# A rebuilt prologue, and kernel sums issued one chunk behind their phase factors, in an S4 convolution with a gated FFN and its backward pass

## The chip, the core and the metric

The kernel runs on one core of one Trainium2 chip. The core has five engines with a queue each: TensorE (PE, with its weight loads shown as PEld), VectorE (DVE), ScalarE (ACT), GpSimd (POOL) and SyncE (SP). DMAs are issued from the queues of SP, ACT and POOL and share 16 DMA engines. The metric is the device time of one execution in microseconds, as the median of several runs.

## What is computed

The reference computes a block and all of its gradients. With x of 2048 rows (time) by 576 channels:

```
xn = layernorm(x)
s  = S4(xn)                 # a long convolution per channel
g  = silu(FFN(xn))          # silu(xn w1) * (xn w3), times w2, 4608 hidden
y  = x + s * g
```

The convolution's kernel is generated per channel d from 128 complex modes n:

```
P[d,n,l] = exp(dt[d] * A[d,n] * l)          # A = A_re + i A_im, l = 0..2047
K[d,l]   = Re sum_n C[d,n] P[d,n,l] dt[d] B[d,n]
```

The outputs are y and the gradients with respect to x, A, B, C, log_dt, Dskip, w1, w3 and w2 (13 arrays).

## The kernel before, in words

Each queue runs its instructions in order. A planner puts them in that order when the program is built: each instruction has a due time (set by `self.at`, which counts for all that follows it, and by program order within it), and the planner places, on a clock of its own estimates, the earliest due instruction that is ready by those estimates. So instructions of different phases interleave, and the order is fixed before the chip runs. Buffers come from pools on a stack. A pool that is opened after another was closed takes over its bytes or its PSUM banks, and its first writer waits for the last reader of the tile that was there.

**Prologue** (no `self.at`, so it is due before all else). It consists of:

- `setup_consts`: identities, constant columns, index row.
- `phase2_params`: loads dt, Dskip and the six matrices A, B, C (576 x 128 each, on 128 partitions x 5 chunks x 128). It computes rho = dt A_re, thp = dt A_im / 2 pi, and W = C B dt (Wr, Wi: ten DVE operations of 128 x 640, two of them sums). W is transposed by PE (L248) and copied by ACT (L251) to `WrT` and `nWiT`. `split_rates` cuts thr, th64 (phase rates modulo one, for steps of 1 and 64) and rho into three bf16 pieces each (L304, L307), and writes them to DRAM as `PCS_dram` with 54 DMAs, alternating between SP and ACT (L81, called from L311).
- `build_selectors`: SEL and SELR, the right-hand sides that turn rates into phases (48 of 128 rows for SELR's use), from integer ramps of POOL (L333 to L337).
- `phase1_layernorm`: 16 tiles of 128 rows are loaded by SP (L135), statistics, root and normalisation on DVE and ACT, 80 transposes on PE (L156) and ten copies out (L159 ACT, L161 DVE) to `xnT`.
- `build_dft_mats`: the 512-point DFT tables dC, dSf, dSi, by DVE and three ACT activations (L539 to L541).
- `ssm_early`: loads the rho pieces as `lhs_r` (L400). For each of 36 chunks of 16 channels, three matmuls on 48 rows of 512 columns (L408) give the exponents, one ACT exponential of 1536 columns (L410) gives the decay factors, and one DMA writes them to `E_dram` (L411). Then, for 32 groups, eight matmuls of 288 columns (L419) give the spectra of xn; DVE copies them out (L423), through a single PSUM buffer, and eight DMAs write `UH_dram` (L425).

**Kernel generation** (`ssm_kernel`, 36 chunks, 8 due-time units apart). Per chunk: phase pieces `lhs_t` (L448, every sixth chunk) and E are loaded; PE makes phases (L466), DVE masks them into `m_k` (L467), ACT makes sine and cosine (`trig`, L316 to L320), DVE multiplies by E to `q_k` and `p_k` (L473, L475), POOL rearranges p into `pz_k` (L482), DVE negates a part (L483) and multiplies by W to `t_k` and `v_k` (L490 to L494). Then 64 small matmuls (L499) sum q times v over the modes into `kps`, and ACT copies that into `KT` (L502). **The FFN** (`ffn_hidden`, from L686) is due beside it: 144 steps of ten matmuls of 512 columns (L719 to L721) with copies on ACT and DVE. The convolution (`ssm_conv`) follows the last chunk; then come the FFN's output, the backward pass and the gradients, which the change leaves alone.

Of the kernel before, what the change touches and what calls it, by code (L numbers as in the profile page):

```python
# [60 lines left out]
class K:  # L61
# [24 lines left out]
    def setup_consts(self):  # L86
# [15 lines left out]
        self.zero_col = const.tile([P, 1], FP32, name="zero_col")  # L102
        nc.vector.memset(self.zero_col[:], 0.0)
# [4 lines left out]
        self.pmod64 = const.tile([P, 1], FP32, name="pmod64")  # L108
        nc.vector.tensor_scalar(out=self.pmod64[:], in0=self.pcol[:], scalar1=64.0, scalar2=-64.0,
                                op0=ALU.is_ge, op1=ALU.mult)  # L110
        nc.vector.tensor_tensor(out=self.pmod64[:], in0=self.pmod64[:], in1=self.pcol[:], op=ALU.add)
# [7 lines left out]
    def phase1_layernorm(self, xp):  # L119
        nc, cfg = self.nc, self.cfg  # L120
        L, D, LT, DT = cfg.L, cfg.D, cfg.LT, cfg.DT
        self.xn_bf = self.persist.tile([P, LT, D], BF16, name="xn_bf")
        self.rstd = self.persist.tile([P, LT], FP32, name="rstd")
        self.xnT = xp.tile([P, DT, L], BF16, name="xnT")
        xf = self.aps["A_u"].flatten_outer_dims()
        half = D // 2
        nfull = D // P
        rem = D - nfull * P
        with self.tc.tile_pool(name="ln_sb", bufs=1) as sb, self.tc.tile_pool(name="ln_small", bufs=4) as small, \
                self.tc.tile_pool(name="ln_ps", bufs=2, space=bass.MemoryType.PSUM) as ps:  # L130
            xs = []
            mv = sb.tile([P, LT, 2], FP32, name="mv")
            for i in range(LT):
                xt = sb.tile([P, D], BF16, name=f"xt{i}")
                nc.sync.dma_start(out=xt[:], in_=xf[i * P:(i + 1) * P, :])  # L135
                xs.append(xt)
                stats = small.tile([P, 2, 6], FP32, name="stats")
                nc.vector.bn_stats(stats[:, 0, :], xt[:, 0:half])
                nc.vector.bn_stats(stats[:, 1, :], xt[:, half:D])
                nc.vector.bn_aggr(mv[:, i, :], stats[:])  # L140
            sd = sb.tile([P, LT], FP32, name="sd")
            nc.scalar.activation(out=sd[:], in_=mv[:, :, 1], func=ACT.Sqrt, bias=self.eps_col[:], scale=1.0)
            nc.vector.reciprocal(out=self.rstd[:], in_=sd[:])
            negmr = sb.tile([P, LT], FP32, name="negmr")
            nc.vector.scalar_tensor_tensor(out=negmr[:], in0=mv[:, :, 0], scalar=-1.0, in1=self.rstd[:], op0=ALU.mult,
                                           op1=ALU.mult)
            for i in range(LT):
                nc.vector.tensor_scalar(out=self.xn_bf[:, i, :], in0=xs[i][:], scalar1=self.rstd[:, i:i + 1],
                                        scalar2=negmr[:, i:i + 1], op0=ALU.mult, op1=ALU.add)
            TB = 8  # L150
            for tb in range(0, LT, TB):
                tsl = slice(tb * P, (tb + TB) * P)
                for c, (do, dsz) in enumerate(cfg.dch):
                    pt = ps.tile([P, TB * P], BF16, name="ln_pt")
                    for j in range(TB):
                        nc.tensor.transpose(pt[:dsz, j * P:(j + 1) * P], self.xn_bf[:, tb + j, do:do + dsz],  # L156
                                            self.ident_bf[:])
                    if c % 2 == 0:
                        nc.scalar.copy(out=self.xnT[:dsz, c, tsl], in_=pt[:dsz, :])  # L159
                    else:  # L160
                        nc.vector.tensor_copy(out=self.xnT[:dsz, c, tsl], in_=pt[:dsz, :])  # L161
                nc.sync.dma_start(out=self.xnT[rem:P, nfull, tsl], in_=self.xnT[0:rem, nfull, tsl])
# [48 lines left out]
    def phase2_params(self):  # L211
        nc, cfg = self.nc, self.cfg
        D, DT, N = cfg.D, cfg.DT, cfg.N
        aps = self.aps
        self.parp_ctx = ExitStack()
        self.parp = self.parp_ctx.enter_context(self.tc.tile_pool(name="parp", bufs=1))
        pp = self.parp
        with self.tc.tile_pool(name="par_tmp", bufs=1) as tmp, \
                self.tc.tile_pool(name="par_ps", bufs=2, space=bass.MemoryType.PSUM) as ps:
# [3 lines left out]
            self.dskip_col = self.load_dvec(pp, aps["A_Dskip"], "dskip", fill=0.0)  # L223
            self.load_rates(tmp)
            dt_b = self.dt_col[:, :, None].to_broadcast([P, DT, N])
            self.rho = tmp.tile([P, DT, N], FP32, name="rho")
            nc.vector.tensor_tensor(out=self.rho[:], in0=self.A_re[:], in1=dt_b, op=ALU.mult)
            self.thp = tmp.tile([P, DT, N], FP32, name="thp")
            nc.vector.scalar_tensor_tensor(out=self.thp[:], in0=self.A_im[:], scalar=1.0 / (2 * PI), in1=dt_b,
                                           op0=ALU.mult, op1=ALU.mult)  # L230
            self.Wr = tmp.tile([P, DT, N], FP32, name="Wr")
            self.Wi = tmp.tile([P, DT, N], FP32, name="Wi")
            t1 = tmp.tile([P, DT, N], FP32, name="t1")
            t2 = tmp.tile([P, DT, N], FP32, name="t2")
            nc.vector.tensor_tensor(out=t1[:], in0=self.C_re[:], in1=self.B_re[:], op=ALU.mult)
            nc.vector.tensor_tensor(out=t2[:], in0=self.C_im[:], in1=self.B_im[:], op=ALU.mult)
            nc.vector.tensor_tensor(out=self.Wr[:], in0=t1[:], in1=t2[:], op=ALU.subtract)
            nc.vector.tensor_tensor(out=self.Wr[:], in0=self.Wr[:], in1=dt_b, op=ALU.mult)
            nc.vector.tensor_tensor(out=t1[:], in0=self.C_re[:], in1=self.B_im[:], op=ALU.mult)
            nc.vector.tensor_tensor(out=t2[:], in0=self.C_im[:], in1=self.B_re[:], op=ALU.mult)  # L240
            nc.vector.tensor_tensor(out=self.Wi[:], in0=t1[:], in1=t2[:], op=ALU.add)
            nc.vector.tensor_tensor(out=self.Wi[:], in0=self.Wi[:], in1=dt_b, op=ALU.mult)
            self.WrT = pp.tile([P, D], BF16, name="WrT")
            self.nWiT = pp.tile([P, D], BF16, name="nWiT")
            for src, dst, sc in ((self.Wr, self.WrT, 1.0), (self.Wi, self.nWiT, -1.0)):
                for c, (do, dsz) in enumerate(cfg.dch):
                    pt = ps.tile([P, P], FP32, name="pt")
# [5 lines left out]
            self.split_rates(tmp)  # L253
            self.dskip_diag = pp.tile([P, DT, P], BF16, name="dskip_diag")
            for c in range(DT):
                nc.vector.tensor_scalar(out=self.dskip_diag[:, c, :], in0=self.ident_bf[:],
                                        scalar1=self.dskip_col[:, c:c + 1], scalar2=None, op0=ALU.mult)
        self.Wr = None
        self.Wi = None
# [28 lines left out]
    def split_rates(self, tmp):  # L288
        nc, cfg = self.nc, self.cfg
        D, DT, N = cfg.D, cfg.DT, cfg.N  # L290
        self.PCS_dram = self.dram.tile([3, 3, D, N], BF16, name="PCS_dram")
        t = tmp.tile([P, DT, N], FP32, name="sr_t")
        thr = tmp.tile([P, DT, N], FP32, name="thr")
        nc.vector.tensor_scalar(out=t[:], in0=self.thp[:], scalar1=MAGIC, scalar2=-MAGIC, op0=ALU.add, op1=ALU.add)
        nc.vector.tensor_tensor(out=thr[:], in0=self.thp[:], in1=t[:], op=ALU.subtract)
        th64 = tmp.tile([P, DT, N], FP32, name="th64")
        nc.vector.tensor_scalar(out=t[:], in0=thr[:], scalar1=64.0, scalar2=MAGIC, op0=ALU.mult, op1=ALU.add)
        nc.vector.tensor_scalar(out=t[:], in0=t[:], scalar1=-MAGIC, scalar2=None, op0=ALU.add)
        nc.vector.scalar_tensor_tensor(out=th64[:], in0=thr[:], scalar=64.0, in1=t[:], op0=ALU.mult, op1=ALU.subtract)
        for q, src in enumerate((thr, th64, self.rho)):  # L300
            pc = tmp.tile([P, 3, DT, N], BF16, name=f"pc{q}")
            r = src
# [1042 lines left out]
```

## Time and profile before

| what | value |
|---|---|
| median of 3 runs | 2397.93 us (2394.15 to 2408.3) |
| the profiled execution | 2408.83 us, its span 2407.0 us |
| busy share of the span | PE 83%, DVE 63%, ACT 38%, POOL 18% |
| mean granted clock of PE | 0.895 |

The profile is of one execution. The span runs from its first to its last instruction; the profiled execution is 1.8 us longer than its span. Shares of busy time are means over stages with different limits. PEld overlaps PE. The granted clock is that of TensorE as a share of full speed. In a row of grouped instructions the figures behind the count are the total busy time and the mean of one in ns, then the idle time of the engine just before them with what ended it. Lines such as L408 are lines of the kernel before.

### The profile page before, as it was taken

What the parts mean: (1) busy time and instruction counts of PE and PEld (TensorE: products, weight loads), DVE (VectorE), ACT (ScalarE), POOL (GpSimd) and SP (SyncE); (2) the same over time, 40 slices, a digit from 0 to 9 for tenths busy, and PEclk for the clock granted to TensorE, in tenths of its full rate; (3) what the DMA queues carried; (4) which work ended last, traced back from release to release, by engine and by line L of the source; (5) the groups of instructions that cost most, each with busy time, mean ns of one, the idle gap of its engine ahead of it and who ended that gap; (6) DMA issues with size and microseconds to landing.
All of it is one profiled execution on the core that took longest, in us unless ns stands there. A gap on an engine that the chain in (4) does not pass through costs nothing.

```text
span 2407.0 us, 42210 instructions
## 1 busy us (share of the span) xinstructions
PE 2008.8 (83%) x16735; PEld 1340.2 (56%) x16790; DVE 1505.0 (63%) x2860; ACT 902.7 (38%) x1461; POOL 426.5 (18%) x691
## 2 busy tenths in 40 slices
PE   0698888788999499789888857989899996799968
PEld 0323333333455277567767745766666675577746
DVE  6414777767788345479969674866655772276751
ACT  0355777667655211254454422333344330000000
POOL 1001444444311211111111111111111111000000
PEclk9656888888899799899999977999999998899989
DMA  3145667566755888755556478667556656999884
GB/s 81 46 192 201 242 230 251 200 226 213 243 193 179 195 219 193 183 145 155 145 148 186 125 123 203 159 176 171 154 163 156 165 140 150 224 193 184 151 115 96
DMA packets 615894, 416.10 MB, mean 173 GB/s; under 512 B 420176, under 2 KB 559568, under 8 KB 610576
## 3 DMA queue, kind: packets, MB, share of 16 engines
q1 hardware_dynamic: 477728, 235.69, 40.7%
q0 software_dynamic: 29520, 109.15, 14.4%
q10 hardware_dynamic: 108448, 68.57, 10.4%
q8 instruction: 131, 2.15, 0.4%
q14 instruction: 67, 0.55, 0.1%
HBM read 130.65 MB, written 190.37 MB: 133 GB/s over the span
## 4 chain that ended last, share of the span: by engine, by line
PE 29%; DVE 13%; issue 12%; DMA 10%; SPq 4%; ACT 4%; POOL 2%; ACTq 1%; POOLq 0%; DVEq 0%
PE px L1214 10%; SPq L1091 4%; PE ph L1133 4%; PE et_ps L578 2%; DMA out_dram<-gw 2%; PE pgw L1170 2%; PE et_ps L940 2%; DMA w2T<-w2r 2%; PE et_ps L560 2%; PE pgw L1159 2%; PE pg L719 1%; PE pu L719 1%; DVE cm_t L602 1%; DVE gg_n L1119 1%; DMA gK<-gK_dram 1%
## 5 line engine op out<-in xcount | busy, mean ns | idle before, releaser
L947 DVE TENSOR_TENSOR pr_q<-et_ps,pz 128x512 f32<-128x512 f32 x288 | 186.0, 680 | 186.0 <-PE et_ps L940 185.9
L1170 PEld LDWEIGHTS <-xn_bf 128*128 128x128 bf16 x2304 | 233.4, 102 | 80.4 <-issue 43.8
L1214 PE MATMUL px<-wTB_w,ggc 128*128 128x288 bf16 x1152 | 243.1, 292 | 33.7 <-DVE gx L1217 11.0
L1214 PE MATMUL px<-wTB_w,guc 128*128 128x288 bf16 x1152 | 242.6, 291 | 23.2 <-DMA guc<-GU_dram 12.1
L719 PEld LDWEIGHTS <-xnT 128*128 128x128 bf16 x1152 | 109.7, 104 | 201.1 <-issue 113.0
L719 PE MATMUL pg<-wmB_w,xnT 128*128 128x512 bf16 x539 | 169.1, 422 | 22.0 <-ACT g_t L727 12.3
L950 DVE TENSOR_REDUCE S_all<-pr_q 128x8 f32<-128x512 f32 x288 | 184.7, 676 | 0.3
L1133 PE MATMUL ph<-w2T,goT 128*128 128x256 bf16 x1152 | 174.5, 284 | 7.2 <-DMA w2T<-w2r 6.7
L1170 PE MATMUL pgw<-gg_n,xn_bf 128*128 128x256 bf16 x1152 | 143.6, 287 | 32.9 <-ACT gw L1173 32.8
L719 PE MATMUL pu<-wmB_w,xnT 128*128 128x512 bf16 x559 | 167.5, 408 | 1.7 <-issue 0.6
L1159 PE MATMUL pgw<-go_o,h_n 128*128 128x288 bf16 x1152 | 165.7, 301 | 1.8 <-ACT gw L1163 1.8
L774 PE MATMUL po<-w2g,hc 128*128 128x288 bf16 x1152 | 146.4, 289 | 20.1 <-DMA w2g<-in_B_w_dram 20.1
L1133 PEld LDWEIGHTS <-goT 128*128 128x128 bf16 x1152 | 99.5, 100 | 96.3 <-issue 62.3
L1214 PEld LDWEIGHTS <-ggc 128*128 128x128 bf16 x1152 | 113.2, 100 | 68.9 <-issue 26.4
L1136 ACT CAST gh<-ph 128x512 bf16<-128x512 f32 x144 | 79.7, 591 | 182.1 <-DMA GU_dram<-gu_n 63.0
L1214 PEld LDWEIGHTS <-guc 128*128 128x128 bf16 x1152 | 114.4, 99 | 56.2 <-DMA guc<-GU_dram 13.5
L1170 PE MATMUL pgw<-gu_n,xn_bf 128*128 128x256 bf16 x1152 | 141.3, 281 | 3.9 <-ACT gw L1163 3.9
L1173 ACT CAST gw<-pgw 128x256 bf16<-128x256 f32 x144 | 51.2, 380 | 248.4 <-DMA out_dram<-gw 104.0
L774 PEld LDWEIGHTS <-hc 128*128 128x128 bf16 x1152 | 112.3, 99 | 50.6 <-issue 20.9
L1159 PEld LDWEIGHTS <-h_n 128*128 128x128 bf16 x1152 | 115.2, 103 | 40.7 <-issue 5.0
L733 POOL DMA_DIRECT2D G_dram<-g_t x72 | 52.5, 728 | 465.7 <-ACT g_t L727 226.5
L1231 ACT ACTIVATE t<-gx 128x576 f32<-128x576 f32 x16 | 10.9, 684 | 324.7 <-DVE gx L1217 299.5
(309 smaller groups left out, 3982.1 us busy)
## 6 DMA issues: line engine op xcount, KB each, us to landing
Q_dram<-q_k SPq DMA_DIRECT2D x36, 512.0 KB, 3.3
G_dram<-g_t POOLq DMA_DIRECT2D x72, 256.0 KB, 3.5
H_dram<-h_t SPq DMA_DIRECT2D x72, 256.0 KB, 3.4
U_dram<-u_t POOLq DMA_DIRECT2D x72, 256.0 KB, 4.0
gg_n<-G_dram POOLq DMA_DIRECT2D x18, 1024.0 KB, 5.4
h_n<-U_dram POOLq DMA_DIRECT2D x18, 1024.0 KB, 6.6
GU_dram<-gu_n ACTq DMA_DIRECT2D x144, 128.0 KB, 3.1
GG_dram<-gg_n ACTq DMA_DIRECT2D x144, 128.0 KB, 4.4
```

Of the source, the lines that this page charges most:

```text
L719: nc.tensor.matmul(pt[:], lhsT=xnT[:, c, ts], rhs=wm[w][:, c, :], start=(c == 0), stop=False)
L733: nc.gpsimd.dma_start(out=dst[fb * ng:(fb + 1) * ng, :, i0:i0 + NT, :].rearrange("g p t f -> p g (t f)"), in_=src[:].rearrange("p g t f -> ...
L774: nc.tensor.matmul(po_[:, pi_, 0:pw], lhsT=hc[:, fi, :], rhs=w2[fi][:, po:po + pw], start=(fi == 0), stop=(fi == FT - 1))
L947: nc.vector.tensor_tensor(out=pr[:], in0=T[h][:].rearrange("p r d k a -> p (r d) k a"), in1=pz[:, dg, h, s:s + 2].rearrange("p r d a -> p ...
L950: nc.vector.tensor_reduce(out=S_all[:, 2 * s:2 * s + 2, d0:d0 + 4].rearrange("p k d -> p d k"), in_=pr[:].rearrange("p (r d) k a -> p d k ...
L1091: self.nc.sync.dma_start_transpose(out=dst, in_=src)
L1133: nc.tensor.matmul(ph[j][:, k, :].rearrange("p (a f) -> p a f", f=P), lhsT=lw, rhs=rh, start=(n == 0), stop=(n == nfull))
L1136: nc.scalar.copy(out=gh[:, j], in_=ph[j][:])
L1159: nc.tensor.matmul(pgw[pi_][:, 0:pw], lhsT=hn[:, tt, fl * P:(fl + 1) * P], rhs=go_o[:, tt, po:po + pw], start=(tt == 0), stop=(tt == LT - 1))
L1170: nc.tensor.matmul(pw_[:, 0:FG], lhsT=self.xn_bf[:, tt, c * P:(c + 1) * P], rhs=nat[:, tt, :], start=(tt == 0), stop=(tt == LT - 1))
L1173: nc.scalar.copy(out=gw[:], in_=pw_[:, 0:FG])
L1214: nc.tensor.matmul(px[pi_][:, 0:pw], lhsT=act[:, fi, :], rhs=wT[part][ai][:, f, po:po + pw], start=(fi == 0 and ai == 0), stop=(fi == FT - ...
```

## The change

The prologue becomes one function, `prologue`. All of its SBUF pools are open at once, so nothing in it reuses another's bytes; two PSUM pools, for the transposes of W and of the LayerNorm, are closed before the pool of the exponentials is opened.

- Order in the program: loads of dt, the matrices and Dskip; selectors; rho and its split; the 16 input loads; the load of `LR_`; LayerNorm; DFT tables; W; exponentials; spectra; then thp, thr, th64 and their splits; dskip_diag.
- Each of the three splits writes its pieces with 6 DMAs for 18 before.
- Wr, Wi, SEL and dskip_diag move from DVE to POOL.
- The exponentials use all 128 rows, the rows from 48 on of `LR_` being set to zero by POOL. They are done in 54 activations of 1024 columns for 36 of 1536, and written with 18 DMAs for 36.
- The spectra have two PSUM buffers for one.
- In kernel generation the sum of a chunk is issued in the program behind the next chunk's instructions, and q and v get three buffers in place of two.

```diff
+            logdt = self.load_dvec(tmp, aps["A_log_dt"], "logdt", fill=0.0)
+            self.load_rates(tmp)
+            dskip_col = self.load_dvec(tmp, aps["A_Dskip"], "dskip", fill=0.0)
+            SELR = self.build_selectors(st, selp)
+            LR_ = lp.tile([P, D // 16, N], BF16, name="lhs_r")
+            nc.gpsimd.memset(LR_[:], 0.0)
...
+            mul(nc.vector, rho, self.A_re, dt_b)
+            self.split3(tmp, rho, 2)
+            self.ln_load(lsb)
+            for k in range(3):
+                nc.sync.dma_start(out=LR_[k * 16:(k + 1) * 16], in_=self.PCS_dram[2, k].rearrange("(k p) n -> p k n", p=16))
+            self.phase1_layernorm(lsb, small, lps)
+            self.build_dft_mats(matp, dg)
...
+            pl = nc.gpsimd
+            for (W, xr, xi, op) in ((Wr, self.B_re, self.B_im, ALU.subtract), (Wi, self.B_im, self.B_re, ALU.add)):
+                mul(pl, W, self.C_re, xr[:])
+                mul(pl, t1, self.C_im, xi[:])
+                pl.tensor_tensor(out=W[:], in0=W[:], in1=t1[:], op=op)
+                mul(pl, W, W, dt_b)
...
+            early.close()
+            eps = late.enter_context(pool(name="ex_ps", bufs=2, space=PS))
+            self.early_exps(SELR, LR_, ep, eps)
+            self.early_spectra(up, ups)
...
+            self.split3(tmp, thr, 0)
+            self.split3(tmp, th64, 1)
...
+        for (c, p0, n, h, d1) in self.dsplit():
+            self.dma(self.PCS_dram[q].rearrange("k (d h) n -> h d k n", h=2)[h, d1:d1 + n], pc[p0:p0 + n, :, c, :])
...
+        for c2 in range(0, NCH, 2):
+            E = ep.tile([P, 2, TW], BF16, name="E_k")
+            Ef = E[:].rearrange("p c t -> p (c t)")
+            for o in range(0, 2 * TW, 1024):
+                pe = ps.tile([P, 1024], FP32, name="e_ps")
+                for k in range(2):
+                    ch, o1 = divmod(o + 512 * k, TW)
+                    nc.tensor.matmul(pe[:, 512 * k:512 * k + 512], lhsT=LR_[:, c2 + ch, :], rhs=SELR[:, o1:o1 + 512],
+                                     start=True, stop=True)
+                nc.scalar.activation(out=Ef[:, o:o + 1024], in_=pe[:], func=ACT.Exp)
+            nc.sync.dma_start(out=self.E_dram[c2:c2 + 2].rearrange("c p t -> p c t"), in_=E[:])
...
-                self.kgen_chunk(ch, E, LT_[:, ch % GE, :], self.SEL, mp, sb, sb, ps, ps1)
...
+                qv = self.kgen_chunk(ch, E, LT_[:, ch % GE, :], self.SEL, mp, sb, qvp, ps)
+                if ch > 0:
+                    self.kgen_sum(ch - 1, prev, ps1)
+                prev = qv
+            self.at(T0 + TK * NCH)
+            self.kgen_sum(NCH - 1, prev, ps1)
```

More of the change, by code (lines that the diff above doesn't have):

```diff
@@ L128, in phase1_layernorm @@
         rem = D - nfull * P
[L129 to L162, printed above, removed]
@@ new lines, in phase1_layernorm @@
+        xs = self.xs
+        mv = sb.tile([P, LT, 2], FP32, name="mv")
+        for i in range(LT):
+            stats = small.tile([P, 2, 6], FP32, name="stats")
+            nc.vector.bn_stats(stats[:, 0, :], xs[i][:, 0:half])
+            nc.vector.bn_stats(stats[:, 1, :], xs[i][:, half:D])
+            nc.vector.bn_aggr(mv[:, i, :], stats[:])
+        sd = sb.tile([P, LT], FP32, name="sd")
+        nc.scalar.activation(out=sd[:], in_=mv[:, :, 1], func=ACT.Sqrt, bias=self.eps_col[:], scale=1.0)
@@ new lines, in phase1_layernorm @@
+        TB = 8
+        for tb in range(0, LT, TB):
+            tsl = slice(tb * P, (tb + TB) * P)
+            for c, (do, dsz) in enumerate(cfg.dch):
+                pt = ps.tile([P, TB * P], BF16, name="ln_pt")
+                for j in range(TB):
+                    nc.tensor.transpose(pt[:dsz, j * P:(j + 1) * P], self.xn_bf[:, tb + j, do:do + dsz],
+                                        self.ident_bf[:])
+                if c % 2 == 0:
+                    nc.scalar.copy(out=self.xnT[:dsz, c, tsl], in_=pt[:dsz, :])
+                else:
+                    nc.vector.tensor_copy(out=self.xnT[:dsz, c, tsl], in_=pt[:dsz, :])
+            nc.sync.dma_start(out=self.xnT[rem:P, nfull, tsl], in_=self.xnT[0:rem, nfull, tsl])
@@ L236, in phase2_params @@
[L236 to L241, printed above, removed]
@@ L364, in ssm_forward @@
+        for (sl, rr) in ((slice(0, QW), rq), (slice(QW, QW + PW), rp)):
+            nc.gpsimd.tensor_scalar(out=self.SEL[:, sl], in0=val[:, sl], scalar1=rr[:, 0:1], scalar2=rc[:, 0:1],
+                                    op0=ALU.mult, op1=ALU.add)
+        return SELR
     def ssm_forward(self, T0, TK, TC):
@@ L412, in ssm_early @@
+        if True:
             for h in range(2):
```

252 lines of the change are left out of this document (118 added, 134 removed).

## The prediction

> **What bounds the kernel now.** I read the busy time by stretch first, because the edits touch only two stages and a share of the whole span says nothing about them.
>
> ```profile
> core 0: us, PE busy (x) PEld busy (x) DVE busy (x) ACT busy (x) POOL busy (x), PEclk, DMA share, GB/s
> 0.00:86.00 86.00, 13.30 (x90) 8.56 (x90) 57.38 (x162) 18.84 (x26) 6.55 (x18) 0.95 0.25 60
> 86.00:111.60 25.60, 18.62 (x72) 10.15 (x72) 6.06 (x8) 0.14 (x1) 0.00 (x0) 0.50 0.29 57
> 111.60:204.00 92.40, 90.76 (x261) 27.37 (x261) 15.15 (x20) 53.48 (x38) 0.00 (x0) 0.50 0.46 181
> 204.00:216.00 12.00, 8.46 (x33) 4.52 (x32) 3.03 (x5) 1.21 (x1) 0.00 (x0) 0.50 0.49 169
> 225.00:620.00 395.00, 324.49 (x3194) 140.70 (x3227) 290.57 (x509) 285.09 (x374) 173.35 (x236) 0.87 0.65 223
> 634.00:820.00 186.00, 170.38 (x1128) 93.01 (x1144) 145.99 (x179) 95.53 (x208) 35.91 (x51) 0.97 0.66 192
> ```
>
> Each row is one stretch; after the five engines come the granted clock, the DMA share and GB/s. The prologue lasts to 216. Its first 86 us have no full engine: a chain. From 111.6 to 204 PE is busy throughout at clock 0.50, so PE sets the pace there. In 225:620 (kernel generation beside the FFN) no engine is full: PE 82%, DVE 74%, ACT 72%; the stage is made of waits. 634:820 is PE at 92% and is not touched.
>
> The timelines (start, length, instruction, wait) show how the prologue chain hangs together.
>
> ```profile
> 5.86 0.53 SPq L81 DMA_DIRECT2D C_im_bf<-in_A_C_im_dram  x1
> 17.75 14.79 SPq L81 DMA_DIRECT2D PCS_dram<-pc  x27
> 32.65 4.38 SPq L448 DMA_DIRECT2D lhs_t<-PCS_dram  x9
> 44.78 7.61 SPq L135 DMA_DIRECT2D xt<-in_A_u_dram  x16
> 47.06 0.46 DVE L138 BATCH_NORM_STATS2 stats<-xt 128x6 f32<-128x288 bf16 x1 [2.42 <-DMA xt<-in_A_u_dram]
> 75.50 1.01 ACT L159 COPY xnT<-ln_pt 64x1024 bf16<-64x1024 bf16 x1 [0.69 <-PE ln_pt L156]
> 84.14 2.00 ACT L541 ACTIVATE dC<-dft_q,halfpi_col 128x2048 bf16<-128x2048 f32 x1
> 86.21 1.39 SPq L400 DMA_DIRECT2D lhs_r<-PCS_dram x3
> 121.28 1.46 PE L408 MATMUL e_ps<-SELR,lhs_r 48*128 48x512 bf16 x3
> 122.67 1.14 PE L419 MATMUL u_ps<-xn_bf,dC 128*128 128x288 bf16 x4
> 123.61 0.45 PE L419 MATMUL u_ps<-xn_bf,dSf 128*128 128x288 bf16 x1
> 216.23 0.63 PE L719 MATMUL pg<-wmB_w,xnT 128*128 128x512 bf16 x1
> ```
>
> SP writes the split rates (27 DMAs, as many on ACT's queue), loads lhs_t, and only then, at 44.78, the input; LayerNorm runs 47.1 to 76.5; the DFT tables end at 86.1; the rates for the exponentials load at 86.2, when the tables' pool is free; the FFN starts at 216.2.
>
> **Part 1, start and LayerNorm.** In the new order the input DMAs depend on nothing and stand behind the parameter loads alone, which leave SP at 6.4; so the first statistics run near 9. The LayerNorm chain itself took 76.5 - 47.1 = 29.4. In front of it DVE now has the selectors and one split instead of three.
>
> ```profile
> L354 DVE SCALAR_TENSOR_TENSOR val<-dl,pm,val 128x1536 f32<-128x1536 f32 x1 | 1.8, 1818 | 0.0
> L335 DVE CAST dl<-ii 128x1536 f32<-128x1536 int32 x1 | 1.0, 961 | 1.0 <-POOL ii L334 1.0
> L227 DVE TENSOR_TENSOR rho<-A_re_bf,dt_col 128x640 f32<-128x640 bf16 x1 | 0.8, 817 | 0.0
> L304 DVE CAST pc<-rho 128x640 bf16<-128x640 f32 x1 | 0.5, 484 | 0.0
> L482 POOL COPY pz_k<-p_k 128x256 bf16<-128x256 bf16 x138 | 104.0, 796 | 27.3 <-issue 23.8 <-DVE p_k L475 3.3
> L445 POOL MEMSET lhs_t<- 128x768 bf16 x2 | 1.4, 736 | 0.0
> ```
>
> Groups by line: busy time, mean of one, idle before. Selectors: two casts 1.9, val 1.8, SELR and the column-sized ones some 2 at these rates: 6. Rate: rho and two subtractions at 0.82, three casts at 0.48: 4. So LayerNorm ends at 9 + 29.4 + 10 = **48**; at 38 if these 10 fit its gaps.
> The exponentials cannot start earlier than that: their two PSUM buffers take four of eight banks, the spectra's two take the other four, and the four are those of the LayerNorm transposes and W's, whose pools close first. "Overlap" here is the rate path, the loads and the tables, not the exponentials.
> The eight Wr/Wi products leave DVE (8 x 0.82 = 6.5) for POOL, where no row shows a two-input operation. Bounds: DVE's 0.82 each below; above, 640 columns at the copy's rate. The copy takes 796 ns for 256 strided columns, so 2.0 each and 16 in all. I take 16, since that row is POOL's own. With POOL's iotas, SEL's two products and the new LR_ memset (4608 columns; the 768-column one takes 0.74, so 4.4) they end at about 30, and the ten W transposes behind them fit before 48. If that cover fails, 8 us.
>
> ```profile
> L490 DVE TENSOR_TENSOR t_k<-p_k,WrT x36: 677/951/3045, 229.7 to 625.5; 128x1024 bf16<-128x1024 bf16 x36
> ```
>
> This DVE product takes 677 ns at best and 3045 at worst (minimum, median, maximum); POOL's copies run beside it. So W on POOL can stretch DVE's LayerNorm by up to POOL's 16: LayerNorm end 64, the upper bound. The Trainium skill, "SBUF — State Buffer", Who interferes with whom, says that DVE and GpSimd share one port pair under an exclusive lock, and the later one blocks fully. The spread in the row agrees; its time is rival 3.
>
> **Part 2, exponentials and spectra.**
>
> ```profile
> L410 ACT ACTIVATE E_k<-e_ps 128x1536 bf16<-128x1536 f32 x36 | 52.1, 1451 | 37.3 <-PE e_ps L408 37.3
> L159 ACT COPY xnT<-ln_pt 128x1024 bf16<-128x1024 bf16 x4 | 4.0, 1012 | 5.6 <-PE ln_pt L156 5.6
> L410 ACT ACT_TABLE_LOAD x1 | 1.3, 1283 | 27.1 <-PE e_ps L408 27.1
> L423 DVE CAST u_e<-u_ps 128x576 bf16<-128x576 f32 x32 | 24.2, 758 | 107.6 <-PE u_ps L419 107.6
> 840.24 12.54 PE L774 MATMUL po<-w2g,hc 128*128 128x288 bf16 x82 [18.88 <-DMA w2g<-in_B_w_dram]
> 853.95 8.86 PE L774 MATMUL po<-w2g,hc 128*128 128x288 bf16 x71 [1.17 <-DMA w2g<-in_B_w_dram]
> 268.23 1.04 PE L719 MATMUL pg<-wmB_w,xnT 128*128 128x512 bf16 x4
> 269.11 1.03 PE L719 MATMUL pu<-wmB_w,xnT 128*128 128x512 bf16 x4
> 840.00:844.00 4.00, 3.76 (x16) 2.34 (x17) 0.61 (x3) 0.00 (x0) 0.75 (x1) 0.50 1.05 362
> 844.00:848.00 4.00, 4.00 (x31) 2.88 (x29) 0.30 (x2) 0.00 (x0) 0.00 (x0) 0.92 1.04 358
> ```
>
> ACT: 54 exponentials of 1024 columns at 1.01 (the PSUM copy of that size) = 54.6; the tables' three activations about 5.8 (2.00 is dC); two table loads 2.6; six split DMAs on its queue (14.79 / 27 = 0.55 each) 3.3: **66**.
> PE at clock 0.50: from 121.28 to 122.67 three exponential matmuls, 0.46 each, and (123.61 - 122.67) / 4 = 0.235 for each of the spectra's 256: 108 x 0.46 + 256 x 0.235 = 110. At clock 1.0: 0.22 (268.23 to 269.11, four) and 8.86 / 71 = 0.125: 24 + 32 = 56.
> DMA: 0.46 x 92.4 + 0.49 x 12 = 48 us of all engines; 18 are left under ACT's 66 for the remaining split writes. DVE: 24 for the spectra and about 10 for the other two splits.
> So ACT sets the end **if the clock rises**: 48 + 66 = 114, and 4 for in-order losses: the FFN starts at 118, a gain of **98**. Does it rise? In 111.6:204 it stayed at 0.50 with PE 98% busy, but 1.39 of every 1.39 + 8 x 0.235 = 3.3 us were matmuls on 48 rows. L774, all 128 rows, went from 0.50 to 1.00 within 8 us of dense work. The change feeds all 128 rows (48 real, the rest zeros) and double-buffers the spectra's PSUM, which removes the gaps of 86:111.6. I count rows, not values, and take 1.0.
> The Trainium skill, "TensorE: Matmul & The Clock Gate", Part 1, says that about 3.4 us of sustained matmuls lift the clock, and makes no condition of how many rows they use. The 92 us at 0.50 do not agree with it; if rows indeed don't matter, what held the clock there may hold it again, and that is rival 1.
> On PE the spectra stand behind the first exponentials, and on ACT the split DMAs wait for DVE's casts with exponentials behind them; both are prices of lateness, within the 4. SP now carries 18 double-size E writes for 36, same bytes; the FFN weights wait there for the parameters' pool, whose last readers (the theta splits) are hidden by DVE's idle time in the exponentials.
> The removed constants (under 0.5 us) and dskip_diag's move to POOL (1.2 on DVE) have cover on both sides: nothing.
>
> **Part 3, sums one chunk later.**
>
> ```profile
> PE kps L499 <- DVE v_k L493: 54.7, 25, 3.9
> DVE pz_k L483 <- POOL pz_k L482: 43.1, 28, 2.3
> DVE m_k L467 <- PE et_ps L466: 25.0, 15, 3.4
> DVE q_k L473 <- ACT C_k L320: 19.1, 14, 2.4
> ```
>
> Waits in 225:620: total, times, longest. PE stands 54.7 us for the v of the same chunk; FFN matmuls and the next phase factors queue behind, and DVE then waits 25.0 for them. With sums of the previous chunk the first wait goes. DVE's waits on POOL and ACT stay, 62.2. Bounds: nothing gained (the planner still puts a sum where its v becomes ready), up to 65: all of PE's idle, 70.5, less a little. I take half of the PE wait, 27, near DVE's 25.0. q and v get a third buffer, so no new wait on them.
>
> **Sum.** The profiled run took 2408.83 (span 2407.0 and 1.8 around it): 2408.8 - 98 - 27 = 2284. It lies 10.9 above the median 2397.93; on the median's scale **2273**.
>
> **Rivals.**
> 1. The clock stays at 0.50: PE's 110 set the end, 48 + 112 = 160, gain 56: 2398 - 56 - 27 = 2315. For it: 92 busy us at 0.50. Against: L774. 0.16.
> 2. Sums are issued as early as before; no gain there: 2300. For it: the wait shows that PE's order already differs from DVE's pace. 0.15.
> 3. POOL's W products block DVE: LayerNorm ends at 64, not 48, so 2289. For it: the 3045 ns; against: DVE's statistics wait for their input at first anyway (2.42). 0.08.
> 4. It doesn't do what it says: FFN and generation are gated by a late pool, as lhs_r was by the tables. If the theta splits (10 on DVE, DMAs, weight load) run after the spectra, about 20 late: 2293; the worst of it eats the gain. 0.10.
> 5. Slower: the clock in the generation stage. Its PE work is 324.49 x 0.87 = 282 at full clock. Above 395 + 98 = 493 the gain is gone, so from a mean clock under 282 / 493 = 0.57. At 0.50: 564, so 2398 - 98 + 169 = 2469. For it: the narrow sums leave the array nearly empty, and dips to 0.50 exist; against: the idle that precedes them shrinks. 0.05.
>
> **How the numbers follow.** Forecast 0.46. Low: LayerNorm at 38 and the full 65: 2398 - 108 - 65 = 2225. High: half clock and no gain of sums, 2342, rounded to 2345; only rival 5 and the tails lie outside. A change under 0.5% (12 us) can't be told from none. Slower 0.05 (rival 5), within 0.5% 0.02 (the worst of rival 4), faster 0.93.
>
> **What would show it.** First xt load near 7, LayerNorm's last copy near 48; exponentials packed at 1.0 us each on ACT; clock 1.0 within 10 us of the spectra's start; first pg matmul near 118; the wait of PE kps on v_k below 20 and the stage some 27 shorter. Wrong if the clock stays low, if W or a split gates the first exponential, or if another DVE wait takes up the sums' place.

## The result, and the profile after

The changed kernel is faster, by about what was forecast:

| | before | after |
|---|---|---|
| median of four runs, us | 2398.92 (2394.15 to 2408.3) | 2290.56 (2281.82 to 2296.16) |
| ratio | 1 | 0.954, 95% interval 0.9496 to 0.9585 |
| span of the profiled run, us | 2407.0 | 2292.4 |
| mean granted clock in it | 0.895 | 0.922 |

The busy time by stretch comes first again, now with the bounds at which the stages of the changed kernel begin and end.

```profile
core 0: us, PE busy (x) PEld busy (x) DVE busy (x) ACT busy (x) POOL busy (x), PEclk, DMA share, GB/s
0.00:58.00 58.00, 14.58 (x90) 9.42 (x91) 45.28 (x130) 15.28 (x25) 26.33 (x32) 0.99 0.35 74
65.50:119.00 53.50, 53.44 (x320) 32.17 (x321) 19.68 (x26) 50.49 (x55) 0.94 (x2) 0.95 0.83 312
119.00:144.00 25.00, 17.56 (x80) 8.34 (x79) 7.40 (x11) 5.08 (x9) 2.15 (x3) 0.80 0.77 241
157.00:539.00 382.00, 330.00 (x3332) 143.63 (x3332) 290.03 (x508) 278.95 (x370) 184.07 (x237) 0.86 0.69 235
```

The exponentials and spectra, 92.4 us at clock 0.50 before, now take 53.5 at 0.95, with PE full and ACT at 94%. A new stretch of 25 us stands behind them, PE at 70%. The last row is the generation stage from its first sum to its last: PE 86% and clock 0.86, against 82% and 0.87 before.

The timelines of ACT, PE and DVE of the changed kernel give the landmarks (start, length, instruction, wait in front).

```profile
36.34 0.24 ACT L258 ACTIVATE nWiT<-pt 128x64 bf16<-128x64 f32 x1 [0.46 <-PE pt L255]
36.60 1.28 ACT L136 ACT_TABLE_LOAD   x1
55.24 1.91 ACT L557 ACTIVATE dSf<-dft_fr 128x2048 bf16<-128x2048 f32 x1
57.06 0.99 ACT L153 COPY xnT<-ln_pt 64x1024 bf16<-64x1024 bf16 x1
70.83 11.11 ACT L408 ACTIVATE E_k<-e_ps 128x1024 bf16<-128x1024 f32 x12 [2.07 <-PE e_ps L406]
118.11 1.07 ACT L408 ACTIVATE E_k<-e_ps 128x1024 bf16<-128x1024 f32 x1
124.40 1.42 DVE L429 CAST u_e<-u_ps 128x576 bf16<-128x576 f32 x2 [3.64 <-DMA UH_dram<-u_e]
128.98 1.67 PE L737 MATMUL pg<-wmB_w,xnT 128*128 128x512 bf16 x7
134.72 0.37 PE L738 MATMUL pg<-wtail,xnT 64*128 64x512 bf16 x1 [1.97 <-DMA wtail<-in_B_w_dram]
142.11 0.86 PE L478 MATMUL et_ps<-SEL,lhs_t 128*128 128x512 bf16 x3
```

LayerNorm's last copy ends at 58.05 (76.5 before), the exponentials are packed (12 in 11.11 us, 0.93 each) and end at 119.2, the FFN starts at 128.98 (216.2), 87 us earlier. The first phase factors come at 142.1 (215.9), only 74 earlier: behind the first FFN matmuls stand the last spectra's writes, the FFN's weights and the loads of the rates, at 0.77 of the DMA engines. From the first phase factors to the last sum it is then 396 us instead of 417, 21 less, so that the FFN's last matmul comes 96 us earlier (725.7 against 821.4). The two spans differ by 114.6 us, so 19 lie behind the FFN, where the change edits nothing. One wait of ACT there is 14.1 us shorter:

```profile
ACT gh L1136 <- DMA GU_dram<-gu_n: 37.4, 1, 37.4
```

```profile
ACT gh L1154 <- DMA GU_dram<-gu_n: 23.3, 1, 23.3
```

The first row is before, the second after (waits of the stretch; total, times, longest). These 19 us are not shown to come from the change. From the FFN's last matmul to the end of the span the traces of all eleven kernels here take 1562 to 1586 us; 1586 is the kernel before, 1567 the changed one, and one kernel with the changed prologue (both edits undone, below) takes 1584 although its longest wait there is 23.0 us.

The wait that the delayed sums should have removed is still there (waits from the first sum to the last):

```profile
PE kps L517 <- DVE v_k L505: 51.6, 23, 3.7
DVE pz_k L495 <- POOL pz_k L494: 42.7, 33, 1.7
```

It was 57.3 us before, from its own first sum to its last (54.7 in the stretch of the prediction), and is 51.6 now, and yet the stage is 21 us shorter. So two questions go to the chip: what did the delayed sums bring, and why did the clock rise in the prologue?

### The profile page after: what moved, and what is told of

Read it like the earlier page. It is cut to its first block, busy times and chain, and to the rows that moved or that the text cites. A ratio compares the mean times of both kernels' runs of the same rounds, so it can differ in the third digit from the quotient of the medians.

```text
span 2292.4 us, 42164 instructions
## 1 busy us (share of the span) xinstructions
PE 1956.9 (85%) x16790; PEld 1333.6 (58%) x16790; DVE 1498.9 (65%) x2842; ACT 900.5 (39%) x1480; POOL 459.5 (20%) x707
## 4 chain that ended last, share of the span: by engine, by line
PE 31%; DVE 16%; issue 11%; DMA 9%; SPq 4%; ACT 4%; POOL 2%; ACTq 1%; POOLq 0%; DVEq 0%
PE px L1232 10%; PE ph L1151 4%; SPq L1109 4%; PE pgw L1188 3%; PE et_ps L958 3%; PE et_ps L596 2%; PE pgw L1177 2%; DMA w2T<-w2r 2%; DVE cm_t L620 2%; DMA out_dram<-gw 2%; PE et_ps L578 2%; PE pg L737 1%; PE pu L737 1%; DVE gg_n L1137 1%; DVE pr_q L965 1%
## 5 line engine op out<-in xcount | busy, mean ns | idle before, releaser
L737 PE MATMUL pg<-wmB_w,xnT 128*128 128x512 bf16 x576 | 176.0, 425 | 12.0 <-ACT g_t L745 10.7
L737 PE MATMUL pu<-wmB_w,xnT 128*128 128x512 bf16 x576 | 172.1, 412 | 3.7 <-ACT u_t L746 3.7
L1188 PE MATMUL pgw<-gg_n,xn_bf 128*128 128x256 bf16 x1152 | 136.4, 278 | 30.2 <-ACT gw L1191 30.2
L1188 PE MATMUL pgw<-gu_n,xn_bf 128*128 128x256 bf16 x1152 | 142.1, 282 | 4.0 <-ACT gw L1181 3.9
L958 PE MATMUL et_ps<-gK,qT 64*128 64x64 bf16 x1152 | 124.6, 289 | 8.6 <-DVE pr_q L965 7.1
```

The lines of the kernel that those rows point to most:

```text
L737: nc.tensor.matmul(pt[:], lhsT=xnT[:, c, ts], rhs=wm[w][:, c, :], start=(c == 0), stop=False)
L958: nc.tensor.matmul(T[h][:, 1 - k, dd].rearrange("p k (f t) -> p k f t", f=2), lhsT=qT[hs, k, d8, :], rhs=gK[hs, :, :, :, cc * 8 + d8].rear ...
L1188: nc.tensor.matmul(pw_[:, 0:FG], lhsT=self.xn_bf[:, tt, c * P:(c + 1) * P], rhs=nat[:, tt, :], start=(tt == 0), stop=(tt == LT - 1))
```

## Experiments

Ratios are against the kernel before in the same session; 0.001 of it is 2.4 us. The changed kernel's own is 0.954.

**The sums, undone alone.** Everything of the change stays, but each sum is issued within its chunk.

```diff
-                if ch > 0:
-                    self.kgen_sum(ch - 1, prev, ps1)
-                prev = qv
-            self.at(T0 + TK * NCH)
-            self.kgen_sum(NCH - 1, prev, ps1)
+                self.kgen_sum(ch, qv, ps1)
```

> The changed kernel with one thing undone: each kernel-generation sum is issued within its own chunk again (q and v keep three buffers). Theory A, the planner had put the sums where their v comes ready in both versions, so the delay did nothing: time as the changed kernel, 2290 within 8 us; first to last sum 381 us within 6; PE waits for v about 50 us. Rival B, the delay is what made that stage 17 us shorter: time 2305 to 2318 and stage near 398.

Measured: 2317.84 us (2306.64 to 2330.7), ratio 0.9641 (0.9613 to 0.9669), first sum to last 157.2 to 559.4, so 402 us instead of 381. Theory A, to which the unchanged wait had led, falls: the delay is worth 0.0101 x 2400 = 24 us, 21 by the landmarks. The window of the stage and PE's longest waits in it, in this kernel:

```profile
157.00:560.00 403.00, 328.55 (x3295) 146.20 (x3330) 289.51 (x508) 280.11 (x370) 180.29 (x237) 0.85 0.65 221
```

```profile
PE kps L513 <- DVE v_k L501: 62.6, 25, 3.9
PE pg L734 <- issue: 4.1, 9, 0.5
PE et_ps L474 <- DVE m_k L475: 3.5, 10, 0.4
```

PE's idle time is 403 - 328.6 = 74 us here and 382 - 330.0 = 52 with the delay: the 22 us are the gain. Half of them is the wait for v (62.6 to 51.6). The other half is waits of at most 0.5 us in front of FFN matmuls and phase factors, 11 us in all, of which two groups are shown; with the delay no such wait is listed.

**The sums two chunks late.** q and v in four buffers.

```diff
-                self.tc.tile_pool(name="kg_qv", bufs=3) as qvp, \
+                self.tc.tile_pool(name="kg_qv", bufs=4) as qvp, \
...
-                if ch > 0:
-                    self.kgen_sum(ch - 1, prev, ps1)
-                prev = qv
+                if ch == 0:
+                    pend = []
+                pend.append(qv)
+                if ch > 1:
+                    self.kgen_sum(ch - 2, pend.pop(0), ps1)
...
```

> The changed kernel with the sums issued two chunks behind their factors (q and v in four buffers). Theory A, the first chunk of delay was used up by the planner's own order, and only a second one makes the sums really late: PE's wait for v falls below 20 us and the stage from first to last sum is 15 to 35 us shorter than 381, the time 2255 to 2275. Rival B, DVE, POOL and ACT set the pace of the stage whatever PE does: the wait falls but the stage stays within 6 us of 381 and the time within 8 us of 2290; PE then waits for something else, the FFN weights or a buffer.

Measured: 2266.08 us (2252.74 to 2267.96), ratio 0.9408 (0.9381 to 0.9434); first sum to last 155.9 to 507.2, 351 us, 30 less. Theory A holds in time, stage and wait: the planner of the instruction order had used up most of the first chunk. PE's order in the traces shows it (K a sum of 64 narrow matmuls with its number, K(1) and K(63) its first and the others, e a phase factor's matmul, f one of the FFN's):

```
one chunk late:  K20(63) f11 e2 f5 e1 f7 K21(1) f1 K21(63) f12 e3 f10 e2 f5 e3 f5 K22(64) f23 K23(1)
two chunks late: f14 e3 f5 K17(64) f19 e3 K18(64) f19 e3 K19(64) f39 e3 K20(64)
```

With one chunk the gaps between sums are still uneven, and many sums are split (a first matmul alone, one FFN matmul, then the rest). That looks like a sum set where its v comes ready by the planner's own times; these times were not printed. With two chunks the order is nearly even.

But where the 30 us come from is not what either theory said. The windows of the stage and PE's waits in it:

```profile
156.00:508.00 352.00, 303.91 (x3299) 132.96 (x3337) 284.79 (x508) 278.33 (x371) 173.24 (x238) 0.92 0.74 256
```

```profile
PE pg L740 <- DVE g_t L746: 28.1, 24, 3.6
PE kps L520 <- DVE v_k L508: 16.0, 9, 2.9
```

The wait for v falls by 36 us, a new one for DVE's copy of pg takes 28 of them back, and PE's idle time is 352 - 303.9 = 48 us, only 4 less. What fell is PE's busy time, by 26 us, at the same work: 330.0 x 0.86 = 284 us at full clock, and 303.9 x 0.92 = 280. The gain is clock. Counted in windows of 1 us, the clock is below 0.75 in 108 of the stage's 382 us with one chunk of delay, and in 58 of 352 with two.

Two waits of nearly the same length show how. The changed kernel, PE's timeline and behind it windows of 2 us:

```profile
310.98 0.19 PE L517 MATMUL kps<-v_k,q_k 128*64 128x16 bf16 x1 [1.24 <-DVE v_k L505]
311.10 0.39 PE L737 MATMUL pg<-wmB_w,xnT 128*128 128x512 bf16 x1
311.42 1.22 PE L517 MATMUL kps<-v_k,q_k 128*64 128x16 bf16 x63
312.90 1.89 PE L737 MATMUL pg<-wmB_w,xnT 128*128 128x512 bf16 x4
```

```profile
310.00:312.00 2.00, 1.02 (x37) 0.67 (x38) 1.70 (x5) 0.00 (x0) 0.95 (x2) 1.00 0.25 90
312.00:314.00 2.00, 2.00 (x44) 1.07 (x39) 2.00 (x4) 1.32 (x3) 0.72 (x1) 0.72 1.00 236
314.00:316.00 2.00, 2.00 (x6) 0.61 (x4) 0.86 (x2) 1.65 (x2) 0.00 (x0) 0.50 1.02 389
```

With the sums two chunks late, the same two views:

```profile
303.33 1.02 PE L740 MATMUL pg<-wmB_w,xnT 128*128 128x512 bf16 x4 [1.45 <-DVE g_t L746]
```

```profile
302.00:304.00 2.00, 0.67 (x4) 0.32 (x4) 2.00 (x5) 2.00 (x3) 0.66 (x2) 1.00 0.86 311
304.00:306.00 2.00, 2.00 (x11) 0.76 (x10) 2.00 (x5) 1.85 (x3) 1.25 (x2) 1.00 0.95 303
```

The wait of 1.24 us has a sum behind it, 64 matmuls of 16 columns, and the clock falls to 0.50: four FFN matmuls take 1.89 us there and about 1.03 at full clock. The wait of 1.45 us has wide matmuls behind it, and the clock stays at 1.00. Over the whole stage, with the idle time counted from 4 us ahead of a sum to its end: in the changed kernel 21 of 36 sums have over 1 us of it, and the mean clock in the 3 us behind them is 0.59, against 0.94 behind the other 15; with two chunks of delay 7 sums have it. A wait in front of a narrow sum is paid twice, as idle time and as half clock behind it. That is read from two orders of the same work; no kernel was run in which the clock alone was changed.

Wide matmuls are no protection from a longer wait. Over the generation stages of all eleven traces, with PE at full clock before the wait, the clock falls within 3 us behind this many waits (a wait counts as ahead of a sum when a sum's matmul ends it or more than 20 of them start in the 2 us behind it):

| wait | ahead of a sum | ahead of wide matmuls |
|---|---|---|
| 1 to 2 us | 56 of 74 | 6 of 28 |
| 2 to 3 us | 29 of 35 | 12 of 16 |
| over 3 us | 59 of 59 | 4 of 4 |

**The exponentials on 48 rows again, and one buffer for the spectra again,** each alone.

```diff
-                    nc.tensor.matmul(pe[:, 512 * k:512 * k + 512], lhsT=LR_[:, c2 + ch, :], rhs=SELR[:, o1:o1 + 512],
+                    nc.tensor.matmul(pe[:, 512 * k:512 * k + 512], lhsT=LR_[0:48, c2 + ch, :], rhs=SELR[0:48, o1:o1 + 512],
...
```

> The changed kernel with the exponentials' matmuls on 48 rows as before. Theory A, the rows that a matmul uses count for the clock: granted clock 0.50 from 60 us on until the FFN starts, PE needs 110 us for the stage, first FFN matmul near 170, time 2325 to 2340. Rival B, the gaps between matmuls count, not the rows: clock 1.00 from about 70 us, first FFN matmul at 129 within 4, time 2290 within 8.

```diff
-                pool(name="ex_psu", bufs=2, space=PS, side="right") as ups, ExitStack() as late, ExitStack() as early:
+                pool(name="ex_psu", bufs=1, space=PS, side="right") as ups, ExitStack() as late, ExitStack() as early:
```

> The changed kernel with one PSUM buffer for the spectra as before (exponentials still on 128 rows). Theory A, rows count for the clock: it is near 1.00 from about 75 us on all the same, the stage is 0 to 15 us longer because DVE's copies (0.76 us, 32 of them) stand between the tiles, time 2290 to 2305. Rival B, gaps count: clock 0.50 through the stage, first FFN matmul near 170 or later, time 2325 or more.

Measured: on 48 rows 2300.1 us, ratio 0.9559 (0.9534 to 0.9585), first FFN matmul at 136.8; with one buffer 2302.86, ratio 0.9587 (0.9556 to 0.9618), first FFN matmul at 129.3 but first phase factors about 7 us later. Neither ratio can be told apart from 0.954. On 48 rows theory B is the nearer one, though time and first FFN matmul lie 2 and 4 us above its bounds; with one buffer theory A holds. The clock is the point: 1.00 from 72 us on in both. First the row of the kernel on 48 rows, then the changed kernel's:

```profile
78.00:90.00 12.00, 12.00 (x65) 4.43 (x64) 4.05 (x6) 10.85 (x12) 0.00 (x0) 1.00 0.87 330
```

```profile
78.00:90.00 12.00, 12.00 (x76) 7.26 (x75) 4.54 (x6) 11.86 (x14) 0.00 (x0) 1.00 0.97 369
```

So in the changed kernel neither the rows alone nor the gaps alone hold the clock at 0.50. (The 48-row kernel does 65 matmuls where the other does 76 in as full a PE; its first FFN matmul comes 8 us later.)

**Both undone at once, and in the other direction the kernel before with 128 rows alone.** The second edit clears LR_ and takes all rows in the old prologue.

```diff
             LR_ = lp.tile([P, NCH, N], BF16, name="lhs_r")
+            nc.gpsimd.memset(LR_[:], 0.0)
...
-                        nc.tensor.matmul(pe[:, o:o + ow], lhsT=LR_[0:48, ch, :], rhs=self.SELR[0:48, h0 + o:h0 + o + ow],
+                        nc.tensor.matmul(pe[:, o:o + ow], lhsT=LR_[:, ch, :], rhs=self.SELR[:, h0 + o:h0 + o + ow],
...
```

> The changed kernel with both undone at once: 48-row exponential matmuls and one PSUM buffer for the spectra. Each alone left the clock at 1.00 (e3_rows48 and e4_one_spectra_buffer). Theory A, the clock rises after about 4 us of full-row matmuls in a row, and either of the two edits alone gives such a stretch, but with both undone every run of 8 spectra matmuls (1.9 us) is broken by a gap or by 48-row matmuls: clock 0.50 until the spectra end, first FFN matmul at 165 to 185, time 2325 to 2350. Rival B, what held the clock in the kernel before lay elsewhere: clock 1.00 from about 75 us, first FFN matmul before 150, time 2290 to 2315.

> The kernel before with its exponentials' matmuls on all 128 rows (48 real, the rest zeros), nothing else. Theory A, as above: the clock rises within 10 us of the first exponential at 112 us, the stage that took 92 us takes 55 to 65, first FFN matmul near 180 instead of 216, time 2365 to 2380. Rival B, rows do nothing: clock 0.50 until 204, first FFN matmul at 216, time 2395 to 2410.

Measured, in one execution each: both undone 2359.55 us (theory A had 2325 to 2350), first FFN matmul at 169.2; before with 128 rows 2365.34 against 2408.48 (2397.41 to 2416.25) for the kernel before in that session, first FFN matmul at 173.1 instead of 216.2. Windows of the first, then of the second:

```profile
70.00:80.00 10.00, 10.00 (x28) 2.31 (x28) 1.51 (x2) 6.22 (x7) 0.00 (x0) 0.50 0.37 144
80.00:100.00 20.00, 20.00 (x57) 5.15 (x56) 3.03 (x4) 11.89 (x12) 0.00 (x0) 0.50 0.50 192
100.00:140.00 40.00, 40.00 (x112) 10.41 (x110) 6.06 (x8) 23.77 (x25) 0.00 (x0) 0.50 0.50 190
```

```profile
86.00:111.60 25.60, 18.52 (x73) 10.23 (x73) 6.06 (x8) 0.24 (x1) 3.94 (x1) 0.50 0.28 55
111.60:116.00 4.40, 4.12 (x15) 1.96 (x15) 0.79 (x2) 2.80 (x3) 0.00 (x0) 0.57 0.12 46
116.00:120.00 4.00, 3.90 (x22) 2.11 (x22) 1.48 (x2) 4.00 (x4) 0.00 (x0) 1.00 0.62 251
```

With both undone PE is 100% busy at 0.50; with zeros in 80 more rows the old prologue goes to 1.00 within 4.4 us of the first exponential's matmul. So the clock and the first FFN matmul follow theory A on both sides. In the changed kernel either of the two edits is enough, and the smaller one, a memset and two slices, brings 43 us in the kernel before by itself.

The reason in theory A, a stretch of full-row matmuls in a row, can be put more exactly from the traces. In each of them the clock changes only on a grid of steps of 3.41 us (to within 0.02 us). Count for each step the columns that PE's matmuls stream in it, each column weighted with the rows that the matmul uses, as a share of 128 (rows of zeros count). All eleven traces, from the first recorded change of the clock on:

| row-weighted columns in a step | steps | with clock 1.00 in the next step |
|---|---|---|
| under 2600 | 995 | 0 |
| 2600 to 3200 | 245 | 81 |
| over 3200 | 5976 | 5973 |

One bound near 3040 puts 42 of these 7216 steps on the wrong side; the best bound on columns without the rows misses 121, on PE's busy time 481. With both undone the steps from 70 to 150 us have 1957 to 2876, with PE fully busy. The step ahead of the rise has 4167 in the changed kernel, 3693 on 48 rows, 3100 with one buffer and 3647 in the kernel before with 128 rows. At 1.00 PE streams faster, so the 48-row matmuls then come to 4246 and more (72 to 127 us) and hold the clock that they could not raise. Of the two waits above, the step with the 1.24 us and the narrow sum has 2393, the one with the 1.45 us and the wide matmuls 3470. This is a count over traces that exist; no kernel was built to test the bound.

**A better prologue on top of the late sums.** First the pools alone: LayerNorm's and the tables' SBUF at the bottom, where the FFN's weights load over them, and the exponentials' PSUM opened ahead of LayerNorm's.

```diff
-        with pool(name="par_tmp", bufs=1) as tmp, pool(name="sel_tmp", bufs=1) as st, pool(name="ln_sb", bufs=1) as lsb, \
-                pool(name="ln_small", bufs=4) as small, pool(name="dftgen", bufs=1) as dg, \
+        with pool(name="ln_sb", bufs=1) as lsb, pool(name="ln_small", bufs=4) as small, pool(name="dftgen", bufs=1) as dg, \
+                pool(name="par_tmp", bufs=1) as tmp, pool(name="sel_tmp", bufs=1) as st, \
...
-                pool(name="ex_psu", bufs=2, space=PS, side="right") as ups, ExitStack() as late, ExitStack() as early:
+                pool(name="ex_ps", bufs=2, space=PS, side="right") as eps, ExitStack() as late, ExitStack() as early:
```

> The changed kernel with the sums two chunks late, the prologue's SBUF pools in the order in which they die (LayerNorm's and the tables' at the bottom, so that the FFN's weights load over them), and the exponentials' PSUM opened ahead of LayerNorm's, the spectra's behind it. Theory A, the FFN weights wait for bytes that are read to the end of the prologue; with the new order they land before the spectra end and the first phase factors come near 134 instead of 142: time 2250 to 2262, against 2266 for the late sums alone. Rival B, DMA is busy at 0.9 there, what is loaded earlier delays the E writes by as much: first phase factors at 140 or later, time 2260 to 2272.

Measured: 2259.99 us, ratio 0.9399 (0.9369 to 0.9429); first copy of phase factors at 136.7, against 142.2 with the late sums alone. The landmark moves between the two theories, nearer to A's 134; the time cannot be told from 0.9408, so for the time this is undecided.

Then the exponentials beside LayerNorm, six of them ahead of the square root in ACT's order.

```diff
-        nc.scalar.activation(out=sd[:], in_=mv[:, :, 1], func=ACT.Sqrt, bias=self.eps_col[:], scale=1.0)
+        with self.tc.issue_after(self.last_exp.ins):
+            self.sqrt_i = nc.scalar.activation(out=sd[:], in_=mv[:, :, 1], func=ACT.Sqrt, bias=self.eps_col[:], scale=1.0)
...
+            self.early_exps(SELR, LR_, ep, eps, 0, 4)
             self.phase1_layernorm(lsb, small, lps)
             self.build_dft_mats(matp, dg)
...
+            self.early_exps(SELR, LR_, ep, eps, 4, D // 16)
+            self.early_spectra(up, ups)
...
```

W's products and transposes follow the spectra in the program, with the copies of W on DVE instead of ACT, and the tables' sines are kept behind the square root and the theta splits behind LayerNorm's copies in the same way as the square root.

> As e7_pools_and_sums, and the exponentials begin before LayerNorm is done: six of them are pinned ahead of the square root on ACT, the others fill the gaps between LayerNorm's copies; W's transposes move behind the exponentials. Theory A, the first exponential is near 31 instead of 58, LayerNorm's last copy is within 4 us of 58, and the first FFN matmul comes at 106 to 118 instead of 128: time 2240 to 2256. Rival B, the earlier exponentials only push LayerNorm (its last copy at 65 or later) or the E writes fill the DMA engines: first FFN matmul at 124 or later, time 2258 to 2272.

Measured: 2252.95 us (2238.15 to 2257.73), ratio 0.9355 (0.9323 to 0.9387); first exponential at 35.3, LayerNorm's last copy from 58.9 to 59.9, first FFN matmul at 120.4. The time is in theory A's range, the first FFN matmul between the two theories. It has the lowest ratio here, 0.0185 x 2400 = 44 us under the changed kernel, 32 of them the second chunk of delay. Its exponentials now end at 102, but PE is the bound that is left:

```profile
60.00:120.00 60.00, 57.40 (x347) 35.75 (x352) 33.91 (x58) 41.46 (x45) 1.42 (x2) 0.94 0.82 297
```

**A third chunk of delay** on top of that, still in four buffers: `ch - 3` for `ch - 2`.

> As e8_exps_beside_ln, with the sums three chunks late and still four buffers for q and v. Theory A, what the delay buys is full clock after the narrow sums, and at two chunks most is had (7 to 9 of 36 sums still stand more than 1 us behind idle time, mean clock of the stage 0.95): first to last sum within 8 us of 347, time within 10 us of 2253, since four buffers held for three chunks make DVE's q wait for PE instead. Rival B, each further chunk takes as much as the second did: stage 320 to 335, time 2225 to 2240.

Measured: 2250.86 us, ratio 0.9382 (0.9332 to 0.9432), first sum to last 354 us; the same as with two, as theory A has it. PE's wait for v is gone behind the first sum, and DVE's copy of pg has taken its place:

```profile
PE pg L744 <- DVE g_t L750: 43.1, 25, 3.7
```

These waits stand ahead of wide matmuls, but 11 of the 15 over 1 us are followed by a fall of the clock all the same; its mean over the stage is 0.91, against 0.95 with two chunks.

## Why the prediction held, and where it did not

2273 us were foretold and 2290.56 measured: a gain of 125 us foretold, 108 measured. Step by step:

**LayerNorm's end, 48 foretold, 58.05 measured:** a term that was too small, though inside the prediction's own bounds (38 and 64). The 10 us come from four places (9.7) and from rounding 48.4 to 48. The first statistics start at 12.5, not 9 (+3.5). The selectors and the rate split lengthen the statistics by 8.7 (21.3 us against 12.6), for which 10 had been set (-1.3). The step that failed is that the tables and W had been laid "behind" or beside LayerNorm at no price: ACT's square root stands right behind W's last copy (36.34, then 36.60 in the rows above), and two of DVE's operations for tables and theta stand between rstd and the normalised rows, so that from the last statistics to these it takes 6.1 us instead of 2.5 (+3.6); and in the transposes two of DVE's table operations and ACT's table load and sine stand in front of the last copy (+3.9).

**W on POOL, 16 us foretold, rival 3:** the eight operations (eight in the kernel before too; the ten named there include rho and thp) took 1.25 to 1.76 us each, 11.3 in all, and ended at 32.3; the bounds of 0.82 and 2.0 each held. That they would block DVE's statistics did not come true. While they run, statistics follow each other at the pace of the kernel before, 0.79 us:

```profile
31.06 1.25 POOL L216 TENSOR_TENSOR Wi<-Wi,dt_col 128x640 f32<-128x640 f32 x1
...
31.42 0.41 DVE L133 BATCH_NORM_STATS2 stats<-xt 128x6 f32<-128x288 bf16 x1
32.21 0.41 DVE L133 BATCH_NORM_STATS2 stats<-xt 128x6 f32<-128x288 bf16 x1
```

```profile
58.08 0.40 DVE L139 BATCH_NORM_STATS2 stats<-xt 128x6 f32<-128x288 bf16 x1
58.87 0.41 DVE L139 BATCH_NORM_STATS2 stats<-xt 128x6 f32<-128x288 bf16 x1
```

The second pair is the kernel before. Other operations of DVE did grow beside POOL: the second subtraction of the rate split took 1.65 us beside POOL's SEL, the first 0.77.

**Exponentials and spectra, 66 + 4 us on ACT foretold:** 61.2 us from LayerNorm's end to the last exponential (0.93 to 0.98 each, not 1.01). ACT is nearly packed, as foretold (from 66.8 us on its waits for PE are 2.9 us), but PE is as full (53.44 of 53.50 us), so ACT is not the only bound. The 4 us for in-order losses were too few: the spectra end 10 us later, in part because DVE's casts wait for the writes of earlier spectra (3.64 in the row above). The two misses nearly cancel, and with the 10 us of LayerNorm the FFN starts at 129 instead of 118: gain 87 for 98. Rival 4 (a late pool) has its share behind that, not ahead: the rates of the first phase factors and the FFN's tail weights came last, and the generation stage gained only 74 of the 87.

**The clock, "I count rows, not values":** right in the result (1.00 from 71 us), and right in the reason as far as it goes. Rows filled with zeros do count: the kernel before with 128 rows has full clock from 116 us. But they are not needed in the changed kernel: the two buffers lift the clock on 48 rows too. By the count above, rows and gaps enter one sum, the row-weighted columns of a 3.41 us step, and each of the two edits lifts it over about 3040. Rival 1's half clock came with neither, at 169 us for the first FFN matmul (160 foretold). A rule by PE's busy time alone fits no better than 481 misses in 7216 steps, and PE was 100% busy at 0.50 for 70 us.

The prediction took the 92 us at 0.50 to disagree with the Trainium skill, "TensorE: Matmul & The Clock Gate", Part 1, by which about 3.4 us of sustained matmuls lift the clock. The length agrees with the traces' steps of 3.41 us; what the traces add is that time on few rows counts for less.

**The sums, "With sums of the previous chunk the first wait goes", gain 27:** the size was near (21 by the landmarks, 24 by the ratios), the mechanism was not, so the near size is partly luck. Here the step that failed is the wait itself: it fell from 62.6 to 51.6 and not below 20. Many sums stayed where they were in PE's order, much as rival 2 had it, but half of the 22 us of idle time came from short waits that the prediction had not counted. It took a second chunk to bring the wait down to 16.0, and most of what that gained was clock, which the prediction had weighed only as a risk (rival 5: below 0.57 the change would have been a loss; it was 0.86).

**The sum:** 98 + 27 foretold; by landmarks 74 + 21 = 95 until the last sum, and in the medians 108. The forecast had 24 too much in the prologue and 6 too much in the sums. Some 13 us lie behind those stages, in a part whose length varies by up to 23 us over the kernels here; no run assigns them to the change, and that they bring the total nearer to the forecast is luck.

## What to carry to other kernels

When PE is fully busy at half clock, ask how many columns it streams on how many rows. Zeros in the unused rows of a short contraction, or a second PSUM buffer, took the clock here from 0.50 to 1.00; in the kernel before, a memset and two slices brought the first FFN matmul forward by 43 us. Narrow matmuls are cheap in a dense stream and dear behind a wait of 1 to 2 us, so issue them late enough that they do not stand first in line; behind longer waits wide matmuls lose the clock too. Where a planner sets the order, moving an operation in the program moves it on the engine only as far as the planner lets it: look at the engine's order, not at the source.

## What the runs showed of the hardware

The clock changed only on a grid of 3.41 us steps. After a step with under 2600 row-weighted columns it was 0.50 in all 995 cases, after one with over 3200 it was 1.00 in 5973 of 5976.

A mix of 48-row and 128-row matmuls did not lift the clock in 70 us of a fully busy PE (0.50 throughout), while the same stage of the kernel before, with 80 rows of zeros added, was at 1.00 after 4.4 us. Once the clock was up, the same mix held it there (1.00 from 72 to 130 us).

A wait of 1.24 us ahead of 64 matmuls of 16 columns took the clock to 0.50; one of 1.45 us ahead of wide matmuls left it at 1.00. Of waits of 1 to 2 us, 56 of 74 ahead of such sums and 6 of 28 ahead of wide matmuls were followed by a fall.

A 48-row matmul between 128-row ones is not cheaper than a full one: 65 matmuls in 12 us of a full PE against 76. The trace puts the cost at the change of rows: at full clock the next matmul starts 0.22 instead of 0.12 us behind a spectra matmul when the rows change, and 0.31 instead of 0.22 us behind an exponential's; between two 48-row matmuls it is 0.23 against 0.22.
